# Attention and routed experts on one core: who sends the last output tiles, and where the strays are counted

## The chip, the cores and the metric

The kernel runs on one core of a Trainium2 chip. The metric is the device time of one execution in microseconds (us); lower is better. The core has a matrix engine (TensorE, PE in the profile, with its weight loads as PEld), VectorE (DVE), ScalarE (ACT), GpSimd (POOL) and SyncE (SP), which computes nothing and issues transfers. ACT and POOL can issue transfers too.

## What is computed

A Nystroem attention over 8 batches and 8 heads (576 rows, 64 columns a head, 32 landmarks) makes rows x of 512 numbers; each row then goes to one of 8 experts.

```python
q_lm, k_lm = means of 18 rows each of q and k          # 32 landmarks
A  = softmax(q @ k_lm.T / 8);  Bm = softmax(q_lm @ k_lm.T / 8);  C = softmax(q_lm @ k.T / 8)
Z  = Bm.T / (norm1(Bm) * norminf(Bm))
for _ in range(6):
    Z = 2 * Z - Z @ Bm @ Z
x  = A @ Z @ C @ v                                      # (4608, 512) over all heads
e_idx  = argmax(x @ w_gate);  gate_w = softmax(x @ w_gate)[e_idx];  eom = sigmoid(x @ w_output_gate)
out[row] = gate_w * eom[e_idx] * (relu(x[row] @ w1[e_idx]) @ w2[e_idx])
```

## The kernel before

The eight batches go through three stages. `attend` brings q, k and v and makes A, C and C@v; `solve` does the pseudo-inverse iterations for one or two batches at once; `finish` does the gating of a batch, asks for the weights of the expert that most of its rows chose, and runs the two expert products for all 576 rows. In `finish`, L1123-1132 fold the attention's small matrix into w1 (U), L1133-1157 compute the hidden layer in eight chunks hT (PE, then a copy with relu by ACT or DVE), and L1158-1201 do the second product in five tiles of rows: four of 128 and one of 64. PE sums a tile in a PSUM bank M (L1170, or L1173 for the tile of 64), ACT (L1182) or DVE (L1184) scales it into one of six buffers y, and transfers take it to the output (L1197), four for each tile, one of 32 rows each (of 64 KB; 32 KB in the tile of 64).

Who issues those four is line 1189: SP all of them for batches 0 to 6. In batch 7, the last, SP issues two of a tile of 128, ACT and POOL one each; of the tile of 64 SP and ACT issue two each. A transfer that SP or ACT issues gets one of eight semaphores, in turn over both engines and in the order of the program. It is issued only when the one before it on the same semaphore has landed, whichever of the two engines had issued that one. An engine that waits for this holds up all that stands behind it in its own queue. A buffer y is written again only when the four transfers that read it have landed.

Rows whose expert is not the one most of their batch chose ("strays") are done by a loop at the end, which runs only if there are any. L1213-1218 count them on DVE, after all else; L1222 loads the count into every engine's register, and each engine then branches past the loop.

The order of the work is not that of the code. Each piece is an operation given to a planner (`Plan.op`, L270), with the engines that could do it, an estimated cost on each, and a rank `prio`. `Plan.run` (L312) gives each operation an engine and a start time by those costs and ranks; the program is then written out in that order. Two tables correct it operation by operation: OFF is added to the ranks, SHIFT makes one engine's choice dearer or cheaper. PR and FR hold the base ranks of each batch; SHY, P_PE, FILL and AFF are further settings of the planner. FILL also sets how many matmuls on an idle tile are put in where PE would stand still early on (L611).

Of the kernel before, what the change touches and what calls it, by code (L numbers as in the profile page):

```python
# [28 lines left out]
ADD = mybir.AluOpType.add  # L29
# [42 lines left out]
class Plan:  # L72
# [419 lines left out]
def kernel(  # L492
# [25 lines left out]
    U2 = S // 2  # L518
    UP = NT * 128
    NH = S // 2  # L520
    SHY = 858.8299
    SHYE = 408.6495
    SHYR = -170.871
    SHYB = 510.1469
# [98 lines left out]
    with tc.manual_schedule():  # L623
# [579 lines left out]
        for bs in GROUPS:  # L1203
# [4 lines left out]
            for b in bs:  # L1208
                finish(b)
        for o in P.run():  # L1210
            o.fn(o.eng)
# [102 lines left out]
```

## Time and profile before

| | us |
|---|---|
| three runs: median (lowest to highest) | 247.3 (245.51 to 249.2) |
| the profiled execution, device time | 245.0 |
| its span, from the first to the last instruction | 243.4 |
| PE busy in the span | 227.4 |
| DVE, ACT, POOL busy | 187.3, 143.0, 133.2 |
| mean granted clock of PE | 0.982 |
| transfers issued for the output by SP, ACT, POOL | 150, 6, 4 |

The device time holds 1.6 us around the span. The chain of work that ended last is followed back from the last computing instruction; what SP issues after that is in the timeline of its queue, not in the chain. A queue's own work is marked with a q (SPq, ACTq).

### The profile page before, as it was taken

The numbers are of one execution on the slowest core, as the hardware profiler recorded it, in microseconds if no ns is written. First come the engines' busy times: TensorE is split into PE (matmuls) and PEld (weight loads), VectorE is DVE, ScalarE is ACT, GpSimd is POOL, SyncE is SP. The second block draws the span as 40 slices with busy tenths as digits, with TensorE's granted clock in tenths as the row PEclk, the third lists the DMA queues.
The fourth block names the chain that finished last, engine by engine and source line by source line (L and its number), as shares of the span: only waits on it lengthen the run. The fifth ranks groups of instructions, "written<-read, shape, count | busy, mean of one in ns | idle before, by whom it ended". The sixth has DMA issues, their size and how long they took to land.

```text
span 243.4 us, 10049 instructions
## 1 busy us (share of the span) xinstructions
PE 227.4 (93%) x4158; PEld 140.8 (58%) x4159; DVE 187.3 (77%) x418; ACT 143.0 (59%) x357; POOL 133.2 (55%) x201
## 2 busy tenths in 40 slices
PE   8999989979988999999999999999999999999960
PEld 3767654556655555665566658675666565564530
DVE  3979788996999989899998899987856684544240
ACT  2658664456775859675795755874773282752410
POOL 2268994978599775977733788808330046020030
PEclk9999999988999999999999999999999999999995
DMA  6999987999999998955864775216981279999462
GB/s 238 259 312 298 293 261 219 232 282 312 265 208 242 255 251 253 260 187 127 254 217 119 219 198 147 56 47 102 212 203 36 75 114 226 226 242 239 126 171 62
DMA packets 30993, 48.96 MB, mean 201 GB/s; under 512 B 5408, under 2 KB 22816, under 8 KB 30944
## 3 DMA queue, kind: packets, MB, share of 16 engines
q1 hardware_dynamic: 19808, 37.21, 53.2%
q0 software_dynamic: 10848, 10.75, 27.6%
q8 instruction: 33, 0.54, 1.0%
q10 hardware_dynamic: 288, 0.33, 0.5%
q14 instruction: 16, 0.13, 0.2%
HBM read 61.90 MB, written 9.44 MB: 293 GB/s over the span
## 4 chain that ended last, share of the span: by engine, by line
PE 80%; DVE 11%; ACT 4%; issue 2%; POOL 0%; DVEq 0%; ACTq 0%; POOLq 0%
PE M L1170 19%; PE S L782 11%; PE M L953 9%; PE S L1142 6%; PE M L1153 6%; PE M L611 6%; PE M L823 5%; PE S L812 4%; PE M L1173 3%; PE M L715 3%; PE M L1003 2%; PE S L1127 2%; DVE s L741 2%; DVE sm L799 1%; DVE Tq L729 1%
## 5 line engine op out<-in xcount | busy, mean ns | idle before, releaser
L1170 PE MATMUL M<-w,hT 128*128 128x512 bf16 x256 | 61.6, 379 | 0.2
L1170 PEld LDWEIGHTS <-hT 128*128 128x128 bf16 x256 | 23.9, 99 | 25.3 <-issue 1.9
L618 POOL DMA_DIRECT2D w<-in_moe_w_dram x26 | 13.1, 507 | 30.9 <-DVE M L1075 24.1
L782 PE MATMUL S<-Tk,lm 32*32 32x288 f32 (+1 forms) x448 | 29.5, 405 | 0.1
L782 PE MATMUL S<-Tq,lm 32*32 32x288 f32 (+1 forms) x448 | 28.8, 404 | 0.0
L953 PE MATMUL M<-X 32*32 32x96 f32 (+1 forms) x768 | 24.3, 243 | 2.9 <-ACT X L967 1.4
L858 POOL TENSOR_TENSOR At<-At,sm 128x576 f32<-128x576 f32 x16 | 18.6, 1162 | 13.8 <-DVE sm L856 5.9
L1182 ACT ACTIVATE y<-M,co 128x512 f32<-128x512 f32 (+1 forms) x27 | 17.1, 643 | 12.2 <-PE M L1170 7.6
L953 PEld LDWEIGHTS M<-X 32*32 32x32 f32 x768 | 16.6, 105 | 13.2 <-ACT X L967 5.6
L849 POOL TENSOR_TENSOR At<-At,sm 128x576 f32<-128x576 f32 x16 | 18.6, 1164 | 9.6 <-DVE sm L828 5.3
L1153 PE MATMUL M<-Ab_all,U 128*128 128x288 bf16 x128 | 23.6, 291 | 0.0
L967 ACT ACTIVATE X<-M 128x192 f32<-128x192 f32 (+1 forms) x31 | 11.9, 384 | 15.9 <-PE M L953 15.6
L1142 PE MATMUL S<-Ab_all,U 128*128 128x288 bf16 x128 | 21.0, 286 | 0.1
L639 ACT ACTIVATE hT<-M 128x288 bf16<-128x288 f32 x43 | 16.7, 414 | 6.3 <-PE M L1153 5.5
L743 POOL TENSOR_TENSOR s<-nq 128x576 f32<-128x576 f32 x11 | 15.5, 1410 | 8.7 <-DMA nq<-in_q_dram 8.6
L1184 DVE TENSOR_SCALAR y<-M,co 128x512 f32<-128x512 f32 (+1 forms) x13 | 9.2, 707 | 13.3 <-PE M L1170 7.3
L639 ACT ACTIVATE hT<-S 128x576 bf16<-128x576 f32 x27 | 17.3, 650 | 1.9 <-PE S L1142 1.7
L611 PE MATMUL M<-idle 128*128 128x512 bf16 x62 | 17.0, 422 | 1.1 <-DVE idle L624 1.1
L782 PEld LDWEIGHTS S<-Tk,lm 32*32 32x32 f32 (+1 forms) x448 | 14.8, 104 | 5.5 <-issue 1.3
L744 POOL TENSOR_TENSOR s<-s 128x256 f32<-128x256 f32 x21 | 15.3, 728 | 1.6
L729 DVE STREAM_TRANSPOSE Tk<-nk 128x1152 f32<-128x1152 f32 x12 | 16.1, 1348 | 0.0
L782 PEld LDWEIGHTS S<-Tq,lm 32*32 32x32 f32 (+1 forms) x448 | 14.5, 105 | 2.7
(136 smaller groups left out, 492.3 us busy)
## 6 DMA issues: line engine op xcount, KB each, us to landing
nk<-in_k_dram SPq DMA_DIRECT2D x16, 576.0 KB, 6.2
nq<-in_q_dram SPq DMA_DIRECT2D x16, 576.0 KB, 6.8
nv<-in_v_dram SPq DMA_DIRECT2D x48, 192.0 KB, 5.3
w<-in_moe_w_dram POOLq DMA_DIRECT2D x16, 512.0 KB, 16.3
out_dram<-y SPq DMA_DIRECT2D x120, 64.0 KB, 3.5
w<-in_moe_w_dram POOLq DMA_DIRECT2D x20, 256.0 KB, 8.6
w<-in_moe_w_dram POOLq DMA_DIRECT2D x3, 1024.0 KB
out_dram<-y SPq DMA_DIRECT2D x30, 32.0 KB, 4.6
```

What stands on the lines that cost most here:

```text
L611: nc.tensor.matmul(p_M.tiles[i].rearrange("p (a c) -> p a c", a=4), lhsT=idle, rhs=idle.rearrange("p (a c) -> p a c", a=1).to_broadcast([1 ...
L639: nc.scalar.activation(out=dst(), in_=src(), func=RELU)
L729: P.op({"DVE": 1265}, lambda e, T=Ts[x], n=ns[x], x=x: nc.vector.transpose(out=T.t.rearrange("p j (t r) -> p t j r", r=m) if x == "q" else ...
L743: nc.gpsimd.tensor_tensor(s3.t, n.t[:, :9], n.t[:, 9:], op=ADD)
L782: nc.tensor.matmul(p.t[o * m:(o + 1) * m, n, :U2], lhsT=l_of(lm, wide, 0 if x == "k" else 1, h, n if wide else j), rhs=t_of(Ts[x], x, wide ...
L849: P.op({"POOL": 1115}, lambda e, At=At, st=st: nc.gpsimd.tensor_tensor(At.t, At.t, b_l(st.t[:, 8:8 + g]), op=SUB), r=[st["ax"]], w=[At[0]] ...
L858: P.op({"POOL": 1115}, lambda e, At=At, st=st: nc.gpsimd.tensor_tensor(At.t, At.t, b_l(st.t[:, 32:32 + g]), op=MUL), r=[st["as"]], w=[At[0 ...
L953: nc.tensor.matmul(pN.t[r_, u * W + lo:(u + 1) * W], lhsT=cur.t[r_, u, :m] if it else nx.t[r_, u], rhs=cur.t[r_, u, lo:], start=(it == 0 a ...
L1142: nc.tensor.matmul(ph.t[:, n, :NH], lhsT=Uw.t[:, hf, fc * 128:(fc + 1) * 128], rhs=Ab.t[:, hf, n * NH:(n + 1) * NH], start=(hf == 0), stop ...
L1153: nc.tensor.matmul(ph.t[:, :NH], lhsT=Uw.t[:, hf, fc * 128:(fc + 1) * 128], rhs=Ab.t[:, hf, n * NH:(n + 1) * NH], start=(hf == 0), stop=(h ...
L1170: nc.tensor.matmul(py.t, lhsT=hTs[fc].t[:, i * 128:(i + 1) * 128], rhs=w2.t[:, fc, :], **f)
L1182: nc.scalar.activation(out=y.t[:, :n], in_=py.t[:, :n], func=COPY, scale=com.t[:, i:i + 1])
```

## The change

Three things are done. Batch 6 gives two of its four tiles of 128 rows to ACT, which issues all four transfers of each; in batch 7 SP and ACT issue two transfers of every tile, and POOL none. The count of the strays is an operation of the plan with the rank 200, ready when the eighth batch has counted its rows, where it stood behind everything before. The estimated cost of an issue by SP in batch 7 is 600 ns in place of 490. Then every number of OFF and SHIFT and of the planner's settings is another.

```diff
-        0: 0.633, 1: -4.252, 2: -0.736, 3: 2.194, 4: 0.896, 5: 0.26, 6: -1.474, 7: -1.709, 8: -0.941, 9:
...
-        5: -381, 7: 173, 9: -168, 11: 2212, 14: 172, 16: 5, 18: 76, 23: 278, 26: 274, 34: -72, 43: 587, 45:
+        5: -855, 7: -999, 13: 361, 14: 2056, 15: -2730, 18: -483, 23: -220, 26: 73, 34: -513, 41: -951, 43:
...
-    SHY = 858.8299
-    SHYE = 408.6495
-    SHYR = -170.871
-    SHYB = 510.1469
+    SHY = 910.5591
+    SHYE = 468.0884
+    SHYR = -168.8377
+    SHYB = 330.0292
...
-    P_PE = -36.8679
+    P_PE = -103.514
...
-    FILL = 1.2429
+    FILL = 1.2095
...
-    AFF = 0.2074
+    AFF = 0.2068
...
-        Abs, coms = {}, {}
+        Abs, coms, emvs = {}, {}, []
...
             P.op({"DVE": 800}, route3, r=[pK[0]], w=[emv[0]], prio=pr + .06)
+            emvs.append(emv[0])
...
-                by = ("SP",) * 4 if b < B - 1 else ("SP", "ACT", "POOL", "SP") if tk == 128 else ("SP", "ACT") * 2
+                by = (("SP", "ACT")[b == B - 2 and i % 2],) * 4 if b < B - 1 else ("SP", "ACT", "ACT", "SP")
...
-                                {"SP": nc.sync, "ACT": nc.scalar, "POOL": nc.gpsimd}[e].dma_start(
+                                {"SP": nc.sync, "ACT": nc.scalar}[e].dma_start(
...
-                    P.op({eng: {"SP": 490, "ACT": 440, "POOL": 1000}[eng] * by.count(eng)}, leave, r=[y[0]], prio=fr, lag=2000,
+                    P.op({eng: {"SP": 490 if b < B - 1 else 600, "ACT": 440}[eng] * by.count(eng)}, leave, r=[y[0]], prio=fr, lag=2000,
...
+        def strays_count(e):
+            nc.vector.tensor_tensor(need, em[:1].rearrange("p (a e) -> p a e", a=1).to_broadcast([1, B, E]),
+                                    main_all[:1].rearrange("p (b e) -> p b e", e=1).to_broadcast([1, B, E]), op=ALU.not_equal)
+            nc.vector.scalar_tensor_tensor(out=need, in0=cnt_all[:1], scalar=E - 0.5, in1=need, op0=ALU.is_ge, op1=MUL)
+            nc.vector.tensor_copy(need_i[:, :B * E], need.rearrange("p b e -> p (b e)"))
+            with nc.allow_low_precision("a count of at most 64"):
+                nc.vector.tensor_reduce(need_i[:, B * E:], need.rearrange("p b e -> p (b e)"), axis=X, op=ADD)
+        P.op({"DVE": 850}, strays_count, r=emvs, prio=200.0)
         for o in P.run():
             o.fn(o.eng)
-
-        nc.vector.tensor_tensor(need, em[:1].rearrange("p (a e) -> p a e", a=1).to_broadcast([1, B, E]),
-                                main_all[:1].rearrange("p (b e) -> p b e", e=1).to_broadcast([1, B, E]), op=ALU.not_equal)
...
```

The order of the instructions differs in few places. PE has the same 2,520 matmuls and 62 on the idle tile. Up to the seventh and eighth batch's last iterations (about 185 us in the profile) its order differs in a few small swaps; from there on the tiles of batches 6 and 7 interleave otherwise. Two copies of the attention's matrix (L641, Ab_all) move from ACT to POOL, and a few copies change between ACT and DVE.

SP's queue at its end, before: the last ten rows are four tiles of batch 6 (four transfers each) and the five of batch 7 (two each), and then the load of the count. A y is a buffer, x4 the number of transfers.

```order
L1197 DMA out_dram<-y_158 32x512 x4
L1197 DMA out_dram<-y_154 32x256 x4
L1197 DMA out_dram<-y_159 32x512 x4
L1197 DMA out_dram<-y_155 32x512 x4
L1197 DMA out_dram<-y_157 32x512 x4
L1197 DMA out_dram<-y_156 32x512 x2
L1197 DMA out_dram<-y_158 32x512 x2
L1197 DMA out_dram<-y_154 32x512 x2
L1197 DMA out_dram<-y_159 32x512 x2
L1197 DMA out_dram<-y_155 32x256 x2
L1222 TENSOR_LOAD need_i
```

The same queue after. All five tiles of batch 6 stood in it before; the tile of 64 and two of 128 are left.

```order
L1201 DMA out_dram<-y_156 32x256 x4
L1201 DMA out_dram<-y_158 32x512 x4
L1201 DMA out_dram<-y_159 32x512 x4
L1201 DMA out_dram<-y_154 32x512 x2
L1201 DMA out_dram<-y_155 32x512 x2
L1201 DMA out_dram<-y_156 32x512 x2
L1201 DMA out_dram<-y_158 32x512 x2
L1201 DMA out_dram<-y_157 32x256 x2
L1227 TENSOR_LOAD need_i
```

ACT's queue at its end, before: the last copies of hT, which PE waits for, the scaling of two tiles of batch 7, and six transfers.

```order
L639 ACTIVATE hT_143<-S_164 128x576
L639 ACTIVATE hT_144<-M_166 128x288
L639 ACTIVATE hT_145<-S_165 128x576
L1182 ACTIVATE y_156<-M_167,co_126 128x512
L1197 DMA out_dram<-y_156 32x512
L1197 DMA out_dram<-y_158 32x512
L1197 DMA out_dram<-y_154 32x512
L1182 ACTIVATE y_159<-M_168,co_126 128x512
L1197 DMA out_dram<-y_159 32x512
L1197 DMA out_dram<-y_155 32x256 x2
```

The same queue after. Four transfers of batch 6 stand ahead of the scaling of its tile of 64 and of three copies of hT, four more behind these, and ten of batch 7 follow.

```order
L1186 ACTIVATE y_155<-M_166,co_125 128x512
L1201 DMA out_dram<-y_155 32x512 x4
L1186 ACTIVATE y_156<-M_166,co_125 128x256
L642 ACTIVATE hT_142<-M_166 128x288
L642 ACTIVATE hT_143<-S_164 128x576
L642 ACTIVATE hT_144<-M_166 128x288
L1201 DMA out_dram<-y_157 32x512 x4
L1201 DMA out_dram<-y_154 32x512 x2
L1201 DMA out_dram<-y_155 32x512 x2
L1186 ACTIVATE y_156<-M_168,co_126 128x512
L1201 DMA out_dram<-y_156 32x512 x2
L1186 ACTIVATE y_158<-M_169,co_126 128x512
```

DVE after, where the count of the strays now stands: behind two of the copies of hT for batch 5 and ahead of a third and of the scaling of two tiles of batch 5.

```order
L648 TENSOR_SCALAR hT_151<-S_164 128x576
L648 TENSOR_SCALAR hT_153<-S_165 128x576
L1215 TENSOR_TENSOR need<-em,main_all 1x64
L1217 SCALAR_TENSOR_TENSOR need<-cnt_all,need 1x64
L1218 CAST need_i<-need 1x64
L1220 TENSOR_REDUCE need_i<-need 1x1
L648 TENSOR_SCALAR hT_152<-M_169 128x288
L1188 TENSOR_SCALAR y_157<-M_169,co_124 128x512
L1188 TENSOR_SCALAR y_158<-M_167,co_124 128x512
```

What moved: eight issues of batch 6 from SP to ACT, four of batch 7 from POOL to ACT, and four small instructions of DVE from the end of its queue to a place between the copies of batch 5.

More of the change, by code (lines that the diff above doesn't have):

```diff
@@ L520 @@
     NH = S // 2
-    SHY = 858.8299
-    SHYE = 408.6495
-    SHYR = -170.871
-    SHYB = 510.1469
-    PR = [-23.1335, -19.0121, -12.2415, -10.6243, -5.0704, -3.1694, -0.9118, 3.6179]
-    FR = [-0.4859, 26.0522, 18.0322, 6.0156, 6.3566, 20.451, 13.3666, 13.9701]
+    SHY = 910.5591
+    SHYE = 468.0884
+    SHYR = -168.8377
+    SHYB = 330.0292
+    PR = [-23.4109, -18.8328, -12.3121, -10.3436, -5.0824, -3.5253, -1.4461, 3.4628]
+    FR = [-1.308, 25.9427, 18.3186, 6.4279, 6.2309, 20.0114, 13.7642, 15.6941]
     PET = 2
     WHALF = (0, 1, 4, 6, 7)
-    P_PE = -36.8679
+    P_PE = -103.514
     P_ACT = 0
@@ L1209 @@
                 finish(b)
+        def strays_count(e):
[6 more added lines that the diff above has]
+        P.op({"DVE": 850}, strays_count, r=emvs, prio=200.0)
         for o in P.run():
             o.fn(o.eng)
-        nc.vector.tensor_tensor(need, em[:1].rearrange("p (a e) -> p a e", a=1).to_broadcast([1, B, E]),
-                                main_all[:1].rearrange("p (b e) -> p b e", e=1).to_broadcast([1, B, E]), op=ALU.not_equal)
-        nc.vector.scalar_tensor_tensor(out=need, in0=cnt_all[:1], scalar=E - 0.5, in1=need, op0=ALU.is_ge, op1=MUL)
-        nc.vector.tensor_copy(need_i[:, :B * E], need.rearrange("p b e -> p (b e)"))
-        with nc.allow_low_precision("a count of at most 64"):
-            nc.vector.tensor_reduce(need_i[:, B * E:], need.rearrange("p b e -> p (b e)"), axis=X, op=ADD)
     engines = [mybir.EngineType.PE, mybir.EngineType.Activation, mybir.EngineType.DVE, mybir.EngineType.Pool,
```

322 rows, old and new, of tables (OFF, SHIFT) are left out of this document.

## The prediction

> **What bounds the kernel now.** The page comes first: who is busy, and when.
>
> ```profile
> span 243.4 us, 10049 instructions
> PE 227.4 (93%) x4158; PEld 140.8 (58%) x4159; DVE 187.3 (77%) x418; ACT 143.0 (59%) x357; POOL 133.2 (55%) x201
> PE   8999989979988999999999999999999999999960
> PE 80%; DVE 11%; ACT 4%; issue 2%; POOL 0%; DVEq 0%; ACTq 0%; POOLq 0%
> ```
>
> PE is at nine tenths in nearly every slice but the last two, and holds 80% of the chain. So there are two questions: can PE end earlier, and how long does the kernel last after PE. The busy time in two stretches answers the first, the last pieces of the chain begin the second.
>
> ```profile
> 185.00:235.30 50.30, 50.11 (x458) 28.30 (x458) 25.75 (x69) 21.34 (x45) 9.74 (x17) 1.00 0.81 163
> ...
> 226.00:235.30 9.30, 9.21 (x59) 4.72 (x57) 2.56 (x5) 3.02 (x6) 1.62 (x4) 1.00 0.54 135
> 235.30:240.60 5.30, 0.00 (x0) 0.00 (x0) 1.12 (x5) 0.00 (x0) 0.43 (x1) 0.74 0.55 141
> 240.60:243.40 2.80, 0.00 (x0) 0.00 (x0) 0.00 (x0) 0.00 (x0) 0.00 (x0) 0.50 0.09 25
> ```
> ```profile
> 229.04 5.18 PE M L1170 x24
> 234.22 1.01 PE M L1173 x16
> 235.23 0.04 DVEq L1184
> 235.27 0.05 issue
> 235.31 0.48 DVE y L1184
> 235.80 0.13 DVE need L1213
> ...
> 236.38 0.13 DVE need_i L1218
> ```
>
> In the rows of windows, after the two ends, come the length and the busy time of PE, PEld, DVE, ACT and POOL. From 185 us on, where the order of PE's work changes, PE lacks 0.19 us of 50.30: there is nothing to win, only something to lose. PE ends at 234.22 + 1.01 = 235.23, the last tile y is ready at 235.79, the strays are counted at 236.51; the span ends at 243.4. These last 8.2 us have no computing in them. The timeline of SP's queue shows what they hold; its columns are the start, the length and the number of issues.
>
> ```profile
> 226.17 5.50 SPq L1197 DMA_DIRECT2D out_dram<-y  x12
> ...
> 233.29 4.87 SPq L1197 DMA_DIRECT2D out_dram<-y  x8
> ...
> 237.85 2.70 SPq L1197 DMA_DIRECT2D out_dram<-y  x3
> ```
> ```profile
> L1197 SPq DMA_DIRECT2D out_dram<-y x22: 314/423/1821, 226.2 to 240.1; - x22
> L1197 ACTq DMA_DIRECT2D out_dram<-y x6: 321/328/451, 231.5 to 236.2; - x6
> ...
> DMA to landing us min/median/max: 1.6/1.7/3.5
> ```
> ```profile
> SPq L1197 <- DMA out_dram<-y: 8.0, 8, 2.0
> ```
>
> SP is behind. It issues batch 6's last three tiles until 231.67, one each 5.50 / 12 = 0.46 us, and its last issue ends at 237.85 + 2.70 = 240.55, that is 4.8 us after the last y was ready. The last row, from SP's waits between 205 and 244 us, says that it also stood eight times, 8.0 us together, until an earlier transfer had landed: the shared semaphores. One issue took 1.821 us where the median is 0.423. From SP's last issue to the end of the span are 243.4 - 240.55 = 2.85 us, which hold the landing and the closing.
>
> **The change, part by part.** The sum is made against the profiled execution, 245.0 us (span 243.4 and 1.6 around it), 2.3 below the median of the runs, 247.3; a gain in the tail does not depend on that difference, so I take it off the median.
>
> *SP's load.* Eight issues of batch 6 leave SP, 8 x 0.46 = 3.7 us of its time; batch 7's ten remain. The tail then hangs on the last tile: ready at 235.79, SP and ACT issue two transfers each, 2 x 0.46 = 0.92, and end at 236.7. On both queues some semaphores belong to transfers that the other engine issued less than a landing (1.7) before; I add 0.2 for one such wait, since SP and ACT now run level. Last issue at 236.9, closing 2.85 as before, end of span 239.75: 3.65 us gained. Bounds: with no wait at all and the shortest landing, 236.7 + 1.6 + 1.15 (2.85 less the median landing), 239.45, a gain of 3.95. At the other end, the backlog was over at 231.67, and batch 7's ten issues, which remain, still took SP from the first ready y (230.80 + 0.69 = 231.49, in ACT's rows below) to 240.55, 9.1 us; if they wait as long, the gain is 0, and with one landing more it is a loss of 1.7. I take 3.65, near the upper end, for this reason: a tile of batch 7 now sends four transfers over the eight semaphores where it sent three, so that a transfer waits for one two tiles older. PE makes a tile in 5.18 / 3 = 1.73, two in 3.5, twice a landing; before, ACT's late single transfers stood between SP's.
>
> *ACT's load.* It issues 18 transfers where it issued 6: twelve more at 0.328, 3.9 us. Its tail:
>
> ```profile
> 223.27 0.47 ACT L1182 ACTIVATE y<-M,co 128x256 f32<-128x256 f32 x1 [3.85 <-PE M L1173]
> 224.53 0.69 ACT L1182 ACTIVATE y<-M,co 128x512 f32<-128x512 f32 x1 [0.78 <-PE M L1170]
> ...
> 227.41 0.65 ACT L639 ACTIVATE hT<-S 128x576 bf16<-128x576 f32 x1
> 230.80 0.69 ACT L1182 ACTIVATE y<-M,co 128x512 f32<-128x512 f32 x1 [2.75 <-PE M L1170]
> ```
>
> The idle times in brackets, 3.85 and 0.78 ahead of the copies of hT and 2.75 behind them, are the cover: four issues of batch 6 (1.3 us) go into the first, the others behind the last copy. Cost 0. If the cover goes, because the four wait for semaphores, three copies of hT are late and PE waits for them; that is a rival below.
>
> *POOL.* Its four issues go; it had nothing else to do. 0.
>
> *Strays.* Four small instructions of DVE, from 235.80 to 236.51, move to about 201 us, where DVE is busy less than half of the time:
>
> ```profile
> 200.00:220.00 20.00, 20.00 (x152) 11.64 (x150) 9.43 (x17) 10.21 (x22) 5.47 (x8) 1.00 1.21 230
> ```
> ```profile
> L1222 PEldq TENSOR_LOAD <-need_i x1: 485/485/485, 236.5 to 236.5; - x1
> ...
> L1222 SPq TENSOR_LOAD <-need_i x1: 494/494/494, 240.6 to 240.6; - x1
> ```
>
> They gain nothing by themselves: SP loads the count at 240.6, long after it is there. With SP done at 236.9 they would have been 0.4 us from mattering, which is why they go with the first part.
>
> *Order.* PE does the same matmuls, in the same order up to 185 us. What it lost before that is in its waits and in its clock, the third figure from the end of a window's row:
>
> ```profile
> PE M L953 <- ACT X L967: 1.4, 3, 0.5
> PE M L953 <- issue: 1.0, 2, 0.6
> ```
> ```profile
> 50.00:53.50 3.50, 2.10 (x68) 1.20 (x56) 3.47 (x7) 1.58 (x5) 2.63 (x5) 1.00 1.13 291
> 53.50:56.90 3.40, 3.40 (x34) 2.02 (x34) 2.57 (x5) 1.91 (x4) 2.89 (x3) 0.50 1.15 305
> ```
>
> In 3.5 us PE was 60% busy, and for the next 3.4 us it got half its clock, which cost half of that, 1.7 us. The change takes one step of the iterations (X, L967) from ACT to DVE at this place and leaves the gaps of the others, so I expect the same stretch again: 0, between -1.7 (it stays warm) and +1.7 (another turns cold).
>
> Sum: -3.65 + 0 + 0 + 0 + 0. Profiled 241.3; against the median 247.3 - 3.65 = 243.65, which I write as 243.6, 1.5% faster.
>
> A rule that speaks against the change stands in the Trainium skill, DMA: Bandwidth & Descriptors, section Issuing engines are not separate DMA queues: transfers of all engines share the same sixteen, and spreading them saves the issue time alone, usually small beside the transfer. Here the share of those engines in the tail is 0.54 and 0.55 (the last column but one above), and one issue, 0.46, is a quarter of a landing, 1.7; so the trace has the issues, not the engines, as what is full. By the rule's first half the gain is the 3.7 us of eight issues, by its second about none.
>
> **The rivals.**
>
> *The clock too (faster by over 2%).* If one cold stretch fewer occurs, 1.7 us more are won: 241.9, a gain of 5.35, 2.2%. For it: the moved step of X, and the three runs before lie 1.8 and 1.9 us apart (245.51, 247.3, 249.2), about one cold stretch each, so that their number seems to vary and a new order may change it. Against it: most of the gaps at 50 us remain. The Trainium skill, TensorE: Matmul & The Clock Gate, section What's actually happening, has the clock judged in free-running windows of about 3.4 us, so that the same program meets them differently; the one stretch of 3.4 us here agrees, and the runs' spread would follow.
>
> *The tail keeps its waits.* The semaphores tie ACT to SP as they tied SP to ACT, or the slow issue (1.821 - 0.423 = 1.4) is met again, since nothing in the rows says that it belonged to the place. Then 3.65 - 1.4 = 2.25 is gained, 245.05; with one more landing of 1.7 in the chain only 0.55, 246.75; at the bound of above nothing, 247.3. This is also the case in which the change does not do what it says. For it: eight waits before. Against it: the two tiles between them, above.
>
> *ACT is held up (slower).* ACT's first four issues of batch 6 wait for the semaphores of batch 5's transfers, and so does the buffer that they leave from. These land while the weights arrive, slowly:
>
> ```profile
> DMA to landing us min/median/max: 2.5/4.8/6.7
> ```
>
> (from 205 to 226 us). Behind them stand the scaling of a tile and three copies of hT, and behind those PE. With two such landings in a row, 13.4, and the cover of 3.85 + 0.78 = 4.6, PE would stand 8.8 us: 243.6 + 8.8 = 252.4, slower by 2.1%. From 3.65 us of waiting on it decides the sign. Against it: batch 5's transfers are issued long before, and ACT waited for none of them in the profile.
>
> **How the numbers follow.** The forecast, 243.6, has a chance of 0.42; the clock too, 0.34; the tail keeps its waits, 0.14; ACT held up, 0.10. Two per cent, 4.9 us, is about what a measurement of this kernel can tell from no change. So faster is 0.34, the same 0.42 + 0.14 = 0.56, slower 0.10. The range leaves out ACT held up and some of the ends: below, two cold stretches fewer (the runs' spread) with the tail's upper bound, 247.3 - 3.95 - 3.4 = 239.95, rounded 239.9; above, the third case's 247.3, no gain. The forecast's own range is 243.35 to 245.05, from the tail's upper bound to the slow issue met again.
>
> **What would show it.** In the profile of the changed kernel SP's last issue should end about 1.7 us after PE's last matmul (5.3 before), and the span 4.5 after it (8.2 before). SP should issue 142 transfers for the output, ACT 18, POOL none. ACT's waits for landings should be small before its last copy of hT, and PE lack no more than 0.5 us from 185 us to its end. The step on the clock is wrong if another number of half-clock stretches than one stands there. The prediction fails if PE's end moves by more than 2 us, or if SP still ends over 3 us after PE.

## The result, and the profile after

| | before | after |
|---|---|---|
| median of 20 runs, us | 247.4 (243.67 to 251.04) | 244.0 (241.67 to 248.89) |
| ratio after to before, 95% interval | | 0.989 [0.985, 0.993] |
| the profiled execution, us | 245.0 | 242.5 |
| its span, us | 243.38 | 240.75 |
| end of PE's last matmul, us | 235.23 | 235.29 |
| from there to the end of the span, us | 8.2 | 5.5 |
| issues for the output by SP, ACT, POOL | 150, 6, 4 | 142, 18, 0 |

A ratio is taken over the runs within 1.5% of the fastest run of each kernel, so that it leans on that one run where runs of one kernel spread by 3 to 4%; the median of all runs therefore stands beside it below.

The changed kernel is about 1.1% faster; in the profiled executions PE ends at the same time (0.06 us later), and the whole gain lies behind its end. First the chain of the changed kernel at its end, then the timelines of SP's and ACT's queues.

```profile
233.25 1.03 PE M L1174 x4
234.28 1.01 PE M L1177 x16
```
```profile
235.91 1.54 SPq L1201 DMA_DIRECT2D out_dram<-y  x2
```
```profile
235.04 2.90 ACTq L1201 DMA_DIRECT2D out_dram<-y  x4
```

PE ends at 234.28 + 1.01 = 235.29, as before (235.23). SP issues its last at 237.45 (240.55 before), but now ACT is last, at 235.04 + 2.90 = 237.94, and the span ends 2.8 us later. Four issues of ACT in 2.90 us are 0.72 each. The row by tile says why; it covers 226 to 241 us, and its three figures are the shortest, the median and the longest in ns.

```profile
L1201 SPq DMA_DIRECT2D out_dram<-y x19: 314/420/1127, 225.7 to 236.3; - x19
L1201 ACTq DMA_DIRECT2D out_dram<-y x14: 321/434/1466, 226.4 to 237.5; - x14
```

The medians are 0.42 and 0.43 us, but one issue of ACT took 1.466 and one of SP 1.127, both on the last tile. SP's and ACT's waits from 205 us on:

```profile
SPq L1201 <- DMA out_dram<-y: 5.6, 7, 1.5
```
```profile
ACT y L1186 <- DMA out_dram<-y: 6.0, 1, 6.0
```

SP stood 5.6 us for landings where it stood 8.0. ACT's 6.0 us look like the rival in which ACT is held up; its timeline shows what they are:

```profile
221.12 0.69 ACT L1186 ACTIVATE y<-M,co 128x512 f32<-128x512 f32 x1 [2.17 <-PE M L1174]
221.83 1.99 ACTq L1201 DMA_DIRECT2D out_dram<-y  x4
223.87 0.47 ACT L1186 ACTIVATE y<-M,co 128x256 f32<-128x256 f32 x1 [2.06 <-PE M L1177]
...
226.36 6.27 ACTq L1201 DMA_DIRECT2D out_dram<-y  x8
232.74 0.69 ACT L1186 ACTIVATE y<-M,co 128x512 f32<-128x512 f32 x1 [6.03 <-DMA out_dram<-y]
```
```profile
224.39 0.40 PE L1157 MATMUL M<-Ab_all,U 128*128 128x288 bf16 x2 [0.20 <-ACT y L1186]
```

A queue's issues do not count as busy, so the 6.03 us of idle time hold ACT's own eight issues, from 226.36 to 232.63, with waits of their own between; the scaling behind them follows 0.1 us later. ACT would have idled without them: in e4 below, with four issues at this place, it idles 6.2 us. PE needed none of this. The four issues at 221.83 did cost something: they stand ahead of the scaling of the tile of 64, whose matmuls were over at 223.2, and PE stood 0.20 us for it.

From 185 us on PE lacks 0.85 us, of which 12 matmul records fewer than before (446 and 458) are a part; and the half-clock stretch of 53.5 us is not there (the third figure from the end is the clock):

```profile
53.50:56.90 3.40, 3.40 (x106) 2.33 (x98) 3.40 (x6) 2.82 (x5) 1.40 (x3) 1.00 1.15 296
185.00:235.30 50.30, 49.45 (x446) 27.95 (x454) 27.30 (x73) 20.51 (x44) 7.96 (x12) 1.00 0.84 171
```

### The profile page after: what moved, and what is told of

Same layout as the page of the kernel before. It is cut to its first block, busy times and chain, and to the rows that moved or that the text cites. A ratio compares the mean times of both kernels' runs of the same rounds, so it can differ in the third digit from the quotient of the medians.

```text
span 240.7 us, 10020 instructions
## 1 busy us (share of the span) xinstructions
PE 224.3 (93%) x4134; PEld 139.9 (58%) x4159; DVE 186.7 (78%) x416; ACT 142.4 (59%) x358; POOL 132.0 (55%) x198
## 4 chain that ended last, share of the span: by engine, by line
PE 78%; DVE 11%; ACT 4%; issue 3%; ACTq 1%; POOL 0%; DVEq 0%; POOLq 0%
PE M L1174 18%; PE S L785 10%; PE M L956 9%; PE S L1146 7%; PE M L1157 6%; PE M L614 6%; PE M L826 5%; PE S L815 4%; PE M L718 3%; PE M L1177 3%; PE M L1006 2%; DVE s L744 2%; PE S L1131 2%; DVE sm L802 1%; DVE Tq L732 1%
## 5 line engine op out<-in xcount | busy, mean ns | idle before, releaser
L1174 PE MATMUL M<-w,hT 128*128 128x512 bf16 x232 | 59.1, 379 | 1.8 <-issue 0.5
L956 PE MATMUL M<-X 32*32 32x96 f32 (+1 forms) x768 | 23.7, 241 | 3.1 <-ACT X L970 1.4
L1186 ACT ACTIVATE y<-M,co 128x512 f32<-128x512 f32 (+1 forms) x26 | 16.6, 649 | 12.8 <-DMA out_dram<-y 6.0
L1157 PE MATMUL M<-Ab_all,U 128*128 128x288 bf16 x128 | 22.9, 288 | 0.2 <-ACT y L1186 0.2
L970 ACT ACTIVATE X<-M 128x192 f32<-128x192 f32 (+1 forms) x32 | 12.4, 388 | 16.7 <-PE M L956 16.3
L642 ACT ACTIVATE hT<-S 128x576 bf16<-128x576 f32 x26 | 16.7, 649 | 2.1 <-PE S L1146 1.9
L732 DVE STREAM_TRANSPOSE Tq<-nq 128x1152 f32<-128x1152 f32 x12 | 16.0, 1343 | 0.0
```

The source lines that it names most:

```text
L642: nc.scalar.activation(out=dst(), in_=src(), func=RELU)
L732: P.op({"DVE": 1265}, lambda e, T=Ts[x], n=ns[x], x=x: nc.vector.transpose(out=T.t.rearrange("p j (t r) -> p t j r", r=m) if x == "q" else ...
L956: nc.tensor.matmul(pN.t[r_, u * W + lo:(u + 1) * W], lhsT=cur.t[r_, u, :m] if it else nx.t[r_, u], rhs=cur.t[r_, u, lo:], start=(it == 0 a ...
L1157: nc.tensor.matmul(ph.t[:, :NH], lhsT=Uw.t[:, hf, fc * 128:(fc + 1) * 128], rhs=Ab.t[:, hf, n * NH:(n + 1) * NH], start=(hf == 0), stop=(h ...
L1174: nc.tensor.matmul(py.t, lhsT=hTs[fc].t[:, i * 128:(i + 1) * 128], rhs=w2.t[:, fc, :], **f)
L1186: nc.scalar.activation(out=y.t[:, :n], in_=py.t[:, :n], func=COPY, scale=com.t[:, i:i + 1])
```

## The experiments

All rows name the time from PE's last matmul on a real tile to the end of the span as the tail, from one profiled execution each, and give the end of SP's and ACT's last issue from the same point. Differences in the text are taken before rounding. The ratio is to the kernel before, run on the same chip.

| kernel | tail | SP, ACT last | ratio [95%] | median, before's median |
|---|---|---|---|---|
| before | 8.2 | 5.3, 1.4 | | |
| changed | 5.5 | 2.2, 2.7 | 0.989 [0.985, 0.993] | 244.0, 247.4 |
| e6: the order alone | 8.5 | 5.7, 1.4 | 1.012 [1.008, 1.015] | 247.3, 247.4 |
| e10: all parts, old order | 6.0 | 3.2, 3.2 | 0.991 [0.985, 0.997] | 245.3, 248.5 |
| e4: batch 6 by SP | 8.6 | 5.8, 3.2 | 0.996 [0.988, 1.005] | 247.5, 247.4 |
| e5: POOL in batch 7 | 8.3 | 3.6, 2.6 | 1.001 [0.995, 1.008] | 247.0, 247.4 |
| e3: count last | 6.8 | 1.5, 1.6 | 0.995 [0.990, 1.001] | 245.1, 247.4 |
| e13: batch 6's split alone | 7.3 | 2.0, 1.4 | 0.997 [0.989, 1.005] | 245.5, 247.7 |
| e9: count early alone | 8.5 | 5.6, 2.8 | 1.021 [1.010, 1.032] | 252.1, 248.5 |
| e8: no strays, no branch | 4.3 | 1.5, 1.6 | 0.985 [0.977, 0.994] | 245.0, 248.5 |
| e7: idle matmuls behind | 6.2 | 3.0, 3.5 | 0.985 [0.974, 0.996] | 244.6, 248.5 |
| e11: PE's branch later | 4.3 | 1.5, 1.6 | 0.993 [0.987, 0.998] | 242.5, 248.7 |
| a12: the changed kernel again | 6.2 | 1.5, 1.6 | 0.995 [0.989, 1.001] | 245.0, 248.7 |

The intervals of most kernels overlap, since a single ratio is known to 0.5% (1.2 us) at best. The tails repeat better: the four kernels in which SP has its 150 issues have 8.2 to 8.6. But the changed kernel itself has 5.5 in one profile and 6.2 in another (a12; the section on the slow issue says why), so that a difference from it of less than 0.7 says nothing. The verdicts below go by the tail and the rows in it, and the ratios only say whether they contradict it.

### One part undone: e4, e5, e3

The three start from the changed kernel, with its plan and order. e4 lets SP issue all of batch 6:

```diff
-                                {"SP": nc.sync, "ACT": nc.scalar}[e].dma_start(
+                                (nc.sync if b == B - 2 else {"SP": nc.sync, "ACT": nc.scalar}[e]).dma_start(
```

> The changed kernel, with its plan and its order, but SP issues all of batch 6's tiles again (150 issues for the output by SP, 10 by ACT). Theory of the number of issues (eight issues of 0.46 us are the gain): SP is late by up to 3.7 us at the end, the gain goes: ratio to before 1.00. Theory of the interleaving (the eight waits came from ACT's and POOL's single transfers between SP's in batch 7, and SP has room in between): little is lost, ratio 0.989 to 0.993, with SP's waits for landings no longer than the 5.6 us of the changed kernel. Also ACT's wait of 6.0 us for a landing ahead of a scaling should stay, as it is for a buffer y and not for an issue.

SP is late again: its last issue ends 5.8 us after PE. SP's waits from 205 us on:

```profile
SPq L1201 <- DMA out_dram<-y: 10.2, 9, 3.1
```

Undoing this part costs 3.2 us, near the eight issues (3.7). The waits go up as well, from 5.6 to 10.2, and the agreement is not a clean one: the longest wait, 3.1 us, is for a landing that came 3.6 us after its issue (the median was 1.7 in the tail of the kernel before); the section on the slow issue has the reason. The theory that only the interleaving in batch 7 counts falls; that the number of issues is all there is, the next two decide.

e5 lets POOL issue one transfer of each large tile of batch 7:

```diff
-                                {"SP": nc.sync, "ACT": nc.scalar}[e].dma_start(
+                                (nc.gpsimd if b == B - 1 and tk == 128 and j == 2 else {"SP": nc.sync, "ACT": nc.scalar}[e]).dma_start(
```

> The changed kernel, with its plan and its order, but POOL issues the third transfer of each of batch 7's four tiles of 128 rows, as before; ACT issues one. Theory of the number of issues: SP has as many as in the changed kernel, so the ratio stays 0.989. Theory of the interleaving: POOL's transfers take none of the eight semaphores, so a tile sends three where it sent four, SP meets younger transfers, its waits grow from 5.6 towards 8.0 us, and 1 to 2.5 us are lost: ratio 0.993 to 0.999.

The tail is 8.3 us, though SP has no more issues than in the changed kernel. SP's waits are 7.2 us from 205 us on, and its last issue comes 1.4 us later than in the changed kernel. But SP does not set the end. Here are POOL's instructions behind its branch, and the closing ones of both engines:

```profile
L1238 POOLq EVENT_SEMAPHORE  x6: 17/30/2374, 237.4 to 240.1; - x6
...
L1238 POOLq INC_SWDGE_SEM  x1: 862/862/862, 240.2 to 240.2; - x1
```
```profile
L1314 POOLq DRAIN  x3: 46/107/2843, 241.1 to 244.5; - x3
L1314 SPq DRAIN  x3: 7/7/13, 242.0 to 244.2; - x3
```

POOL issues its last transfer at 236.5, waits 2.374 us for its landing, then counts its queue up (0.86) and drains (2.84), until 243.96. The Trainium skill, Perfetto Trace Analysis, section DMA Instruction — SWDGE (GPSIMD), has the end that the profiler shows for such an issue leave out the movement of the data; the trace agrees, the issue is 0.50 us long and POOL is released 3.6 us after its start. SP comes to its own drain at 242.0 and waits for POOL for 2.1 us. The kernel ends when the last engine has closed, and POOL's closing is longer than SP's. The late landing is not POOL's own: the transfers of SP and ACT in flight at that time took 3.1 to 3.5 us to land (2.8 to 3.4 in the changed kernel), while in e13 below POOL's last transfer, issued at the same place, had landed within 2.6 us.

e3 puts the count of the strays behind everything, as before:

```diff
-        P.op({"DVE": 850}, strays_count, r=emvs, prio=200.0)
+        P.op({"DVE": 850}, lambda e: None, r=emvs, prio=200.0)
         for o in P.run():
             o.fn(o.eng)
+        strays_count("DVE")
```

> The changed kernel, with its plan and its order, but with the count of the strays emitted last, as before. Theory of the slow issues (the last issues of SP and ACT took 1.13 and 1.47 us because PE, which had the count early, branched at 235.4 and so fetched 16 KB of instructions at 236.1, just then): PE now loads the count after 236.5 and branches near 237.5, the fetch comes near 238.3, the last issues take about 0.4 each, SP and ACT issue their last at about 236.9, and the kernel ends some 0.8 to 1.0 us earlier than the changed one: ratio to before about 0.985. Theory that the count's place is free either way (the sum of the prediction): 0.989, as the changed kernel. Theory that the early count carries part of the gain: 0.991 or more, SP's and ACT's load of the count waiting for DVE.

Each theory has half of it. The slow issues are gone and SP and ACT issue their last 1.5 and 1.6 us after PE, as the first said; and yet the tail is 6.8, longer than either of the changed kernel's. It is POOL again. Its closing instructions, then SP's wait (as a wait for the queues' closing):

```profile
L1239 POOLq COMPARE_BRANCH  x1: 53/53/53, 239.1 to 239.1; - x1
...
L1239 POOLq INC_SWDGE_SEM  x1: 787/787/787, 240.1 to 240.1; - x1
```
```profile
L1315 POOLq DRAIN  x3: 40/107/2522, 240.9 to 244.0; - x3
```
```profile
SPq L1315 <- PEq L1315: 2.5, 2, 2.0
```

The row names PE, as the semaphore is that of all engines; PE had been at its own closing since 240.2, and POOL arrives at 243.4. POOL branches when the count is there, about 1.6 us after PE's last matmul, and needs 4.4 us from there to the end of its drain. With the count early its branch is at 213.6 and its drain over at 229. In the kernel before it ended 0.75 us ahead of SP's arrival (241.75 and 242.5), hidden by 8 us of SP:

```profile
L1309 POOLq DRAIN  x3: 46/107/2843, 238.9 to 243.1; - x3
L1309 SPq DRAIN  x3: 7/7/13, 242.5 to 242.8; - x3
```

### One part alone: e13, e9, e6, e10

e13 keeps only the split of batch 6 (the edits of e3 and e5 together):

> The changed kernel's plan and order with one of the three parts alone: batch 6 gives two tiles to ACT, while POOL issues the third transfer of batch 7's tiles and the count of the strays comes last, as before. The prediction's sum (eight issues fewer on SP are 3.65 us, POOL and the count 0): the span ends 4.5 to 5.5 us after PE's last matmul, ratio 0.985 to 0.989. Theory of POOL's closing (it follows the count and POOL's last transfer, and was 0.75 us behind SP's in the kernel before): SP issues its last at 1.5 to 3 us after that matmul, but POOL's closing holds the end, 7.3 to 8.3 us after it; the part alone brings 0 to 0.9 us, ratio 0.996 to 1.000.

The theory of POOL's closing holds. SP ends 2.0 us after PE, 0.2 earlier than in the changed kernel, but the tail is 7.3 us: the part that the prediction gave 3.65 us to brings 0.9 alone (1.2 against e6, which has the same order). SP's row of waits and POOL's drain:

```profile
SPq L1315 <- PEq L1315: 2.8, 2, 2.3
```
```profile
L1315 POOLq DRAIN  x3: 46/107/2843, 239.9 to 243.3; - x3
```

e13 and e3 also price the interleaving by themselves, since in both the count is last and no slow issue meets the last tile: e13 sends three transfers of a tile over the semaphores, e3 four. SP's waits from 205 us on, e13 first:

```profile
SPq L1201 <- DMA out_dram<-y: 6.0, 7, 1.6
```
```profile
SPq L1201 <- DMA out_dram<-y: 5.5, 5, 2.4
```

The difference is 0.5 us in the waits and 0.5 in SP's last issue (2.0 and 1.5). Most of the 1.4 us by which SP is later in e5 is therefore not the interleaving. Batch 7's part alone, without POOL and with the rest as before, was not run.

e9 is the kernel before with only the count early, emitted right behind the last batch's routing:

```diff
+            routes.append(last)
...
         for o in P.run():
             o.fn(o.eng)
+            if o in routes:
+                routes.remove(o)
+                if not routes:
+                    strays_count()
```

> The kernel before, with its order and all its issues, but the count of the strays emitted right behind the routing of the last batch. Theory that SP's late issues alone end the kernel before (the prediction: the count gains nothing by itself): tail of 8.2 us after PE, ratio 1.000. Theory that POOL's closing, which follows the count by about 5.5 us to the end of the span, was a second bound close behind: still 8.2 us, since SP is 0.8 us later than POOL there. Theory that the early count alone brings what undoing it lost (1.3 us): tail 6.9, ratio 0.995.

The tail is 8.5, so the count brings nothing by itself, as predicted. That the kernel is slower (1.021, six runs) was expected by no theory. Two causes show in the trace: between 200 and 220 us, where the count now stands on DVE, PE falls back by another 0.8 us, and two issues on the last tile take over 1.7 us (below). The profiled run also had a half-clock stretch of 6.8 us at 28 us. Whether these make up the whole of 3.6 us in the median stays open.

e6 is the order alone: the edits of e3, e4 and e5 together.

> The changed kernel's order alone: batch 6 by SP, the third transfer of batch 7's tiles by POOL, the count of the strays last, all as before. If the gain is all in the issues (the prediction's sum, order 0): ratio to before 1.000. If the order with its tables brings part of it (it avoids the half-clock stretch at 53.5 us, worth 1.7): 0.993. If the order costs and the issues gain more than they show: 1.003 or more.

The tail is 8.5, near the 8.2 of before. The medians say no difference, the ratio 1.2% slower (it leans on one run of the kernel before at 242.83). There is no sign of a gain.

e10 is the converse, the kernel before with its order and all three parts (the count as in e9):

```diff
-                                {"SP": nc.sync, "ACT": nc.scalar, "POOL": nc.gpsimd}[e].dma_start(
+                                {"SP": nc.scalar if b == B - 2 and i % 2 else nc.sync, "ACT": nc.scalar, "POOL": nc.scalar}[e].dma_start(
```

> The kernel before, with its tables and its order of computing, but with all three parts: two tiles of batch 6 issued by ACT, batch 7's by SP and ACT half each, the count of the strays early. If the three parts are the gain and the order of the new tables none (the prediction's sum): tail of about 5.5 us after PE's last matmul and ratio 0.989. If the new tables are needed, because ACT's issues now stand where nothing planned for them and hold up the last copies of hT: PE ends 1 to 4 us later, ratio 0.993 to 1.005.

0.991 against 0.989, tail 6.0: the three parts are the gain and the new tables are not needed for it, within the interval.

### The slow issue: e8, e7, e11

The packets of the queue that brings instructions are 16 KB each, 33 in an execution for PE's 8,293 matmuls and weight loads, one for about 250, and the last of them begins 0.7 to 1.5 us behind PE's branch in every run that has one; from this I take the queue to be PE's. Here are the times of that last one, from PE's last matmul, in us, with the end of the branch:

```
            PE's branch   fetch            longest of the last issues   last packet of the output
before          2.3       3.2 to 4.5       1.82 (SP)                    6.1
changed         0.1       0.9 to 1.9       1.47 (ACT), 1.13 (SP)        3.5
changed (a12)   0.1       1.6 to 2.6       0.44                         3.9
e3              2.4       3.2 to 4.4       0.43                         2.5
e8            none        none             0.43                         2.5
e7              0.1       0.9 to 2.6       2.24 (ACT), 1.89 (SP)        4.3
e11             2.6       3.3 to 4.7       0.43                         2.5
```

Over the whole execution of the kernel before, 18 issues of SP and ACT took over 0.8 us, and 15 of them overlapped a fetch; in the changed kernel 18 of 20. Of the 36 issues that overlap one, about half are slow (15 and 18), of the 204 and 208 others three and two. In e4, e5, e7, e9 and e10 the branch is early as well, the fetch begins 0.7 to 0.9 us after PE's last matmul, and each has issues of about 1.7 us or more on the last tile.

e8 leaves out the count, its load, the branch and the loop for the strays.

> The changed kernel's plan and order, with the count of the strays, its load, the branch and the loop for the strays left out; with this data the loop has nothing to do. Theory of the fetch after the branch: without a branch no fetch stands at the end, the last issues take 0.4 each and the span ends 4.2 to 4.6 us after PE's last matmul: ratio 0.984 to 0.986. Rival, that the slow issue belongs to the place: 5.0 to 5.5 us. Either way POOL closes early, since it waits for no count.

Tail 4.3, the last issues 0.43. This tells the fetch from the place, but takes away the loop too. e7 was to move the branch alone:

```diff
         for o in P.run():
             o.fn(o.eng)
+        fill(8, 0)
```

> The changed kernel with eight matmuls on the idle tile put behind PE's last real one; they add about 1.7 us to PE's own queue and nothing else reads them. Theory that PE's fetch of instructions after its branch slows the issues in flight: the branch comes at about 1.8 us after the last real matmul instead of 0.1, the fetch at about 2.6 to 3.6, after SP's and ACT's last issues, which then take about 0.4 each; SP's and ACT's last issues end at 1.6 us after PE's last real matmul (2.2 and 2.7 in the changed kernel) and the span 4.5 to 4.8 after it (5.5 in the changed one): ratio to before about 0.986. Theory that the slow issue belongs to the place (the last transfers of a tile of 64 rows): nothing changes, 5.5 us and 0.989.

It did not: eight matmuls and their loads fit into PE's queue, PE's branch was over at 0.1 us, ahead of them, and the slow issues stayed. The kernel tells nothing between the theories. e11 makes PE wait for DVE:

```diff
         for o in P.run():
             o.fn(o.eng)
+        for _ in range(6):
+            nc.vector.memset(idle, 0.0)
+        fill(1, 0)
```

> The changed kernel, with six small writes of the idle tile by DVE behind its last scaling and one matmul on that tile behind them, so that PE has to wait for DVE before it branches; nothing else waits for it. Theory of the fetch after the branch: the branch moves from 0.1 to about 1.9 us after PE's last real matmul, the fetch to about 2.7, behind the last issues, which take 0.4 each; SP and ACT issue their last at 1.5 and 1.6 us after that matmul, as they did without any branch, and the span ends at about 4.3 to 4.6 (5.5 in the changed kernel): some 1.0 us less than the changed kernel on the same chip, ratio to before about 0.985. Theory that leaving out the loop for the strays, and not the fetch, made the difference: 5.5 us, as the changed kernel.

The branch moved, and the loop is still there. The changed kernel's branches, then e11's, then e11's issues of the last tiles:

```profile
L1238 PEldq COMPARE_BRANCH  x1: 358/358/358, 235.0 to 235.0; - x1
```
```profile
L1241 PEldq COMPARE_BRANCH  x1: 353/353/353, 243.5 to 243.5; - x1
```
```profile
L1201 SPq DMA_DIRECT2D out_dram<-y x7: 314/366/423, 239.0 to 242.3; - x7
L1201 ACTq DMA_DIRECT2D out_dram<-y x6: 321/404/520, 239.4 to 242.4; - x6
...
DMA to landing us min/median/max: 1.6/1.8/2.0
```

e11's PE ends at 241.3, so its branch begins 2.2 us behind; the changed kernel's began 0.2 us ahead of that end. No issue takes over 0.52 us, no landing over 2.0, and the tail is 4.3 as without any branch. So the branch is the cause, with the fetch that follows it; which of the two, the next run tells.

> The changed kernel itself, on the chip of the run before, as its measure: span to end 5.4 to 6 us after PE's last matmul, with two issues of over 1 us in it; ratio to before 0.985 to 0.993.

Two issues of over 1 us were expected, and none came. In this execution of the changed kernel the branch stood at the same place, but the fetch came 0.7 us later and met no issue, only the landings: the last packet of the output came 3.9 us after PE, 1.4 later than in e3, e8 and e11, and the tail was 6.2. SP waits for these landings at its closing:

```profile
SPq L1314 <- DMA out_dram<-y: 1.9, 2, 1.7
```

What is disturbed moves with the fetch, not with the branch. A fetch in flight thus costs 1.2 to 1.9 us either way (5.5 and 6.2 against 4.3); how it holds up the transfers, no run shows. e11 is the version to keep: its median is 2.5 us below the changed kernel's on the same chip, of which the tail explains 1.2 to 1.9; the two ratios overlap, and the mean of all runs differs by 1.5 us, with an interval from -3.3 to +0.3.

## Why the prediction was right, point by point

The forecast was 243.6 and the time 244.0; its place, the tail behind PE, was right. The step that failed is the split of the sum over the parts: the whole gain was given to one of them, and the two that were priced at nothing are what lets it show. That the time came within 0.4 us of the forecast is in part luck: the tail gave 2.7 us of the 3.65, and the ratio, 0.989 of 247.4, says 2.7 too; only the medians differ by 3.4.

- *Which bound.* Right. PE's end moved by 0.1 us, the tail by 2.7. SP issues 142 transfers and ACT 18, as said; SP's last comes 2.2 us after PE (1.7 predicted) and the span ends 5.5 after it (4.5 predicted).
- *SP's load, 3.65.* The sum was that of all three parts, not of this one, which brings 0.9 alone (e13). With the fetch out of the way SP and ACT issue their last 1.5 and 1.6 us after PE (1.7 predicted) and the tail is 4.3 (4.5 predicted), in e8 and e11. With the fetch the changed kernel gets 2.7. The 0.2 for a wait was not needed. SP's waits fell as the choice near the upper end had it, from 8.0 to 5.6 us, but the reason given, four transfers a tile on the eight semaphores in place of three, is worth only 0.5 (e13 against e3). The Trainium skill's rule that spreading issues over engines saves the issue time alone (DMA: Bandwidth & Descriptors, section Issuing engines are not separate DMA queues) agrees with e4 in its first half: 3.2 us for eight issues, 3.7 by their time, though a wait of 3.1 us for a late landing stands in e4's tail too.
- *POOL's issues, 0: "it had nothing else to do".* Wrong by 2.1 to 2.8 us (e5 against the two profiles of the changed kernel), of which the landing that the fetch made late is a part. A transfer that POOL issues late also puts off POOL's closing, which was 0.75 us from being the bound before. Where the count holds that closing anyway, POOL's issues cost 0.5 (e13 against e3).
- *Strays, 0 by itself, 0.4 from mattering behind SP.* Right by itself (e9), wrong in the second: with SP no longer late, not SP's load of the count but POOL's closing hangs on it. Against the tail of 4.3 that e11 has with an early count, e3's 6.8 makes 2.5 us; against the changed kernel, which the early branch charges with the fetch, 1.3 or 0.6.
- *The closing of 2.85.* It was taken for SP's own. It is 2.7 to 2.8 when SP or ACT is last (after, e8, e11), 4.6 in a12, where the last landings are late, and 5.2 in e3, where POOL is last.
- *The rival that the slow issue is met again (245.05).* It came, in this mechanism: 2.7 gained instead of 3.65 (2.25 by the rival). The prediction said that nothing in the rows tied the 1.821 us to its place; the packets of the instruction queue did, and they were not read.
- *ACT's load, 0, and ACT held up.* PE lost 0.20 us to four issues ahead of a scaling; no wait of ACT for a landing cost more. The first four went out in 1.99 us, 0.5 each, without the waits for slow landings that the rival needed.
- *Order, 0.* Right on the tail (e6 8.5, e10 6.0) and within about 1% on the times.
- *The clock.* The forecast of one half-clock stretch failed, and so did its reason. It belongs to the run, not to the order. The same changed kernel had none in one profile and one in another (a12), and e9, which has the kernel before's order, had a double one elsewhere:

```profile
74.80:78.20 3.40, 3.36 (x71) 3.22 (x74) 1.99 (x4) 1.20 (x3) 0.83 (x1) 0.60 1.19 249
```
```profile
28.00:31.40 3.40, 2.27 (x23) 1.41 (x22) 0.00 (x0) 0.81 (x2) 3.24 (x5) 0.52 1.05 372
31.40:34.80 3.40, 3.40 (x60) 1.90 (x56) 0.99 (x3) 1.30 (x3) 1.40 (x4) 0.50 0.99 280
```

The stretches are 3.4 us long or twice that, which fits the free-running windows of about 3.4 us that the Trainium skill has (TensorE: Matmul & The Clock Gate, section What's actually happening).

That PE ended at the same time in the two profiles although one had lost 1.7 us to the clock is then a coincidence: the changed kernel's PE was 1.1 to 1.4 us ahead from 63 to 137 us, only 0.4 at 148, behind single gaps, and none at its end; in a12 it ended 3.8 us later (239.1).

## What to carry to other kernels

A kernel ends when its last engine has closed, so follow every engine from its last work through its closing, and take the end of the second latest as the bound on what a change to the latest can bring. An engine's last transfer, or the last value that it waits for, may cost nothing in its busy time and yet hold the end: here POOL's. Where several parts share one end, each can be worth little alone (0.9 and 0 here, of 2.7 together) while undoing any one of them costs more (1.3 to 3.2 against the changed kernel's first profile, 0.6 to 2.4 against its second).

## What the runs showed of the hardware

- PE's instruction fetches, 16 KB in 0.9 to 2.2 us, one for about 250 instructions and one behind a branch, disturb the transfers: an issue of SP or ACT that meets one takes 0.8 to 2.4 us in place of 0.42 about every second time, or, in a12, the output's last packet comes 1.4 us later.
- PE's branch runs ahead of at least eight matmuls with their loads that still stand in its queue (e7).
- POOL's closing after it has issued transfers is 0.8 to 0.9 us of counting and 2.5 to 2.8 us of draining, and begins only when its last transfer has landed (a wait of 2.4 us in e5).
- In 13 profiles of these kernels there is none (four times) or one stretch at half clock ahead of PE's end, 3.4 or about 6.8 us long, beginning between 28 and 76 us.
